# Two heads in one kernel: a weight load split in two, a bank held in the scan's later groups, and a new written-out order

## The chip, the core and the metric

The kernel runs on one core of a Trainium2 chip. The metric is the device time of one execution in microseconds (us). Three runs of the kernel before took 134.9, 135.98 and 136.2 us; their median is 135.98 us.

The core's engines each work through a list of their own, in order: TensorE (PE, with the weight loads as PEld), VectorE (DVE), ScalarE (ACT), GpSimd (POOL) and SyncE (SP). SP issues most DMA transfers, ACT and POOL some.

## What is computed

Two independent heads over sequences of 2048 rows of 448 columns, bfloat16 in and out, side by side in the output:

```
A: dt = exp(log_dt);  Lam_bar = exp(dt * Lam)                    # complex, 448 states
   Bu = x @ (((Lam_bar - 1) / Lam) * B).T
   h[t] = Lam_bar * h[t-1] + Bu[t]                               # scan over 2048 steps
   y = 2 * real(h @ C.T) + x * Dskip

B: q, k, v = split(x @ wqkv), 16 heads of 28
   logits[s, w] = q[s] . k[s - 2w] / sqrt(28),  w = 0..7         # 8 positions back, 2 apart
   o = softmax(logits) @ v,   out = o @ wo
```

## The kernel before

**How the work is cut.** Head B is cut into two halves of 1024 rows, b = 0 and 1. Its q and k are projected in blocks of 128 columns (`prep`: `first` for the two leading blocks of b = 0, in quarters; `proj` for the rest; matmuls at L494 and L453), evicted by ACT into `qk` (by the helper `copy`, L202 without and L204 with a scale), multiplied on DVE for all eight distances (`qk`, L560, tile `prods`), summed over the head's columns by PE with a selection matrix (L573), and put through a softmax (L588 on). v is projected at L673 into `ra` and later `qk`, gets its halo rows by DMA (L699, L701), and DVE forms the weighted sum (`pv`: L727 multiply, L733 add, L736 to L744 fold) in four groups. SP transposes each group (L771), PE applies `wo` (L790, L797), and the result is evicted into `ra` (L804) and stored (L807).

Head A is a chunked scan (`scan`) in seven groups m of 64 complex states, each 128 partitions high. In each group PE forms four inputs from x (L1135), two of them in a bank pair P, the odd ones in a bank each. Then a chain of small steps goes to and fro between PE and ACT: `s1` (L1152), eviction `e1` (L1156), `s2` (L1159), eviction (L1163), `s3` (L1167 to L1169), a second-level scan of five steps (L1179) with evictions `pbuf` (L1174), `s4` (L1185), and the evictions into h (L1188, L1212, L1240). DVE or ACT builds the powers `pw` that serve as weights (L1084, L1082). The outputs of A come from L1319 (seven matmuls per half tile), after a skip term that PE (L1338) or ACT (L1331, from DVE's product L1305) puts into the bank; they are stored at L1342.

**The bank of the odd term.** After `e1` has left bank 1 of a group, the carry must be added to what was in it (`s5`). The table `FIN` says how, per group, for the pair P and for this bank. "seed" means that the bank is given back after `e1`, and that ACT later copies `e1` into a bank (`back1`, L1199) on which `s5` then accumulates. "hold" means that the bank is kept from `s1` to the end of `s5` and its eviction, and no copy back is made. Before, all entries are "seed".

**What sets the order.** A planner has a list of some 610 units, each with its engine, its predecessors and the PSUM banks that it takes and gives back. The order in which the units are issued is written out as numbers in `ORDER` (a number over 1000 takes the unit's second engine), and the bank of each claim in `BANKS`. So an engine's list follows `ORDER`; an engine waits only for what its next instruction needs.

**The weights of q and k.** `loads` fetches `wqkv` in column groups a (0 to 127), b (128 to 255) and c (256 to 447), for rows 0 to 383: a on ACT's queue, b and c on SP's. The last 64 rows come in one transfer on ACT's queue (L362). `shift` then makes a copy of the weights moved by 64 partitions (`copy`: L202 on ACT, L206 on DVE), and `wm` gathers the last 64 columns of q and k (L434, DVE). For the last block the rows of k3 and q3 are copied to the other half of the partitions by DMA (`dup`, L535 and L536), on SP's queue. Eleven warm-up matmuls (L287) open PE's list.

**The tail.** The last output tile of each head is evicted in halves. The second half is shared by ACT (256 columns) and DVE (192 columns); all stores are issued by SP.

Of the kernel before, what the change touches and what calls it, by code (L numbers as in the profile page):

```python
# [16 lines left out]
D = 448  # L17
# [25 lines left out]
FIN = (("seed", "seed"),) * 7  # L43
# [32 lines left out]
]  # L76
BANKS = [
# [235 lines left out]
class PartB:  # L313
# [9 lines left out]
    def loads(self):  # L323
# [38 lines left out]
        nc.scalar.dma_start(self.wqk[0:DT, 3], self.B_wqkv[DF:D, 0:2 * D])  # L362
        nc.scalar.preload_act_table_set("natural_log_exp_and_others")
        self.u_w["a", 0] = P.add("ACTQ", 0.0, lambda: None, lat=4.8)
        self.u_wr = P.add("ACTQ", 0.0, lambda: None, lat=5.7)
        self.u_xh = {}
        for h in range(2):
            for m in range(2):
                self.u_xh[h, m] = P.add("SP", 1.33, lambda h=h, m=m: half(h, m), [self.u0], -9, lat=(3.3, 3.0, 3.2, 2.9)[2 * h + m], dma=1.0)
            c0, c1 = ((NCH, 2 * NCH), (2 * NCH, D))[h]  # L370
            self.u_w["bc"[h], 0] = P.add("SP", 0.95, lambda c0=c0, c1=c1: cols(nc.sync, c0, c1), [self.u0], -9, lat=(3.4, 3.0)[h], dma=(0.9, 1.2)[h])
# [1110 lines left out]
```

## Time and profile before

| | us |
|---|---|
| median of three runs (lowest, highest) | 135.98 (134.9, 136.2) |
| profiled execution, its own time | 135.03 |
| its span, first to last instruction | 133.3 |
| PE, DVE, ACT busy | 126.8, 113.4, 105.4 |
| POOL busy | 12.1 |
| last matmul group starts, last store is issued | 129.00, 130.56 |

The span is what the engines' records cover; 1.7 us of the execution's own time lie around it. An engine's busy time counts its instructions, not DMA issues; a matmul that is in flight counts as busy, so PE's share is no measure of its rate. In a timeline row the first number is the start, the second the length, then engine, line, operation, what it writes and reads, and in brackets how long the engine stood idle before and what released it. In the chain of waits a row names the engine that led at that time.

### The profile page before, as it was taken

The page shows a single profiled execution, that of the slowest core. Times are in us where ns is not written, and L with a number is a line of the kernel's source. Part 1 is how long each engine was busy: PE and PEld are TensorE (multiplying, and loading weights), DVE is VectorE, ACT ScalarE, POOL GpSimd, SP SyncE. Part 2 cuts the span into 40 slices and gives each one's busy share as a digit, 9 for nine tenths or more (in the row PEclk, how much of TensorE's full clock was granted, in tenths as well). Part 3 has the DMA queues.
Part 4 walks back from the last instruction along what each step waited for, and adds up shares of the span by engine and source line. Part 5 has one row for each costly group of instructions (what it writes and reads, how often), then busy time and mean ns, then how long its engine had stood idle before and what let it go on. Part 6 is the DMA issues. An engine that isn't in the chain of part 4 may idle for free.

```text
span 133.3 us, 2479 instructions
## 1 busy us (share of the span) xinstructions
PE 126.8 (95%) x921; PEld 63.4 (48%) x921; DVE 113.4 (85%) x130; ACT 105.4 (79%) x189; POOL 12.1 (9%) x28
## 2 busy tenths in 40 slices
PE   6999989999999999999999899999999999999990
PEld 2477333434546434464454255444566555545430
DVE  5256998999999999999999999999999999992011
ACT  2067968987999957879999999989999649569270
POOL 6940491000000000000000000000000000000000
PEclk9999999999999999999999999999999999999998
DMA  4999949989346758827869988006620685318642
GB/s 91 207 199 186 146 100 232 178 193 201 73 91 104 170 147 290 222 51 152 266 97 143 260 210 244 19 0 138 147 67 0 165 227 199 102 63 219 234 148 93
DMA packets 47759, 20.25 MB, mean 152 GB/s; under 512 B 38774, under 2 KB 46346, under 8 KB 47748
## 3 DMA queue, kind: packets, MB, share of 16 engines
q1 hardware_dynamic: 46676, 19.77, 64.7%
q10 hardware_dynamic: 880, 0.31, 1.2%
q8 instruction: 7, 0.11, 0.4%
q0 software_dynamic: 192, 0.03, 0.1%
q14 instruction: 4, 0.03, 0.1%
HBM read 5.18 MB, written 4.19 MB: 70 GB/s over the span
## 4 chain that ended last, share of the span: by engine, by line
PE 73%; ACT 15%; SPq 5%; DMA 3%; issue 1%; DVE 0%; ACTq 0%
PE banks L1319 16%; PE banks L1135 12%; PE banks L453 10%; PE banks L790 7%; PE banks L673 7%; PE banks L573 6%; SPq L349 4%; PE banks L1179 3%; DMA rb<-in_B_wqkv_dram 3%; ACT qk L202 2%; ACT pbuf L1174 2%; PE banks L1152 2%; ACT h L202 2%; PE banks L797 2%; ACT banks L1217 1%; SPq L360 1%
## 5 line engine op out<-in xcount | busy, mean ns | idle before, releaser
L560 DVE TENSOR_TENSOR prods<-qk 128x4096 bf16<-128x4096 bf16 (+1 forms) x18 | 31.7, 1809 | 0.3 <-ACT qk L202 0.2
L1135 PE MATMUL banks<-xaT_sb,Bcat 128*128 128x512 bf16 (+1 forms) x112 | 26.9, 381 | 0.6 <-ACT h L202 0.6
L202 ACT CAST ra<-banks 128x896 bf16<-128x896 f32 (+2 forms) x24 | 17.9, 773 | 7.8 <-PE banks L797 4.2
L202 ACT CAST qk<-banks 128x512 bf16<-128x512 f32 (+3 forms) x20 | 16.9, 843 | 3.9 <-PE banks L453 1.4
L733 DVE TENSOR_TENSOR prods<-prods 128x7168 bf16<-128x7168 bf16 x4 | 15.6, 3892 | 0.1
L727 DVE TENSOR_TENSOR prods<-ra 128x7168 bf16<-128x7168 bf16 x4 | 15.5, 3886 | 0.0
L727 DVE TENSOR_TENSOR prods<-ra,qk 128x7168 bf16<-128x7168 bf16 x4 | 15.5, 3886 | 0.1
L1319 PE MATMUL banks<-Ccat,h 128*128 128x448 bf16 x64 | 14.7, 353 | 0.0
L453 PE MATMUL banks<-rb 128*128 128x512 bf16 (+1 forms) x64 | 13.3, 379 | 0.6 <-ACT sh L960 0.6
L1135 PEld LDWEIGHTS <-Bcat 128*128 128x128 bf16 (+1 forms) x112 | 9.1, 100 | 9.7 <-issue 3.7
L673 PE MATMUL banks<-wv,rb 128*128 128x448 bf16 (+1 forms) x64 | 13.7, 354 | 0.0
L1319 PE MATMUL banks<-Ccat,qk 128*128 128x448 bf16 x48 | 11.7, 352 | 0.0
L790 PE MATMUL banks<-wo_p,rb 128*128 128x448 bf16 x48 | 10.9, 354 | 0.0
L1174 ACT CAST pbuf<-banks 128x64 bf16<-128x64 f32 (+1 forms) x42 | 9.3, 229 | 0.9 <-PE banks L1179 0.6
L1179 PE MATMUL banks<-pbuf,pw 128*128 128x64 bf16 x77 | 9.7, 235 | 0.2
L204 ACT ACTIVATE qk<-banks 128x512 bf16<-128x512 f32 (+2 forms) x10 | 8.4, 849 | 1.2 <-PE banks L453 1.0
L1179 PEld LDWEIGHTS <-pw 128*128 128x128 bf16 x77 | 6.5, 105 | 5.5 <-issue 1.9
L453 PEld LDWEIGHTS <-rb 128*128 128x128 bf16 (+1 forms) x64 | 5.1, 96 | 7.9 <-issue 2.8
L206 DVE CAST ra<-banks 128x192 bf16<-128x192 f32 x2 | 0.7, 358 | 9.2 <-ACT ra L202 9.2
L1319 PEld LDWEIGHTS <-h 128*128 128x128 bf16 x64 | 5.8, 98 | 5.3 <-issue 0.7
L1084 DVE TENSOR_TENSOR pw<-Dm,spair 128x1280 bf16<-128x1280 bf16 (+1 forms) x13 | 8.0, 664 | 0.0
L1148 ACT CAST eP<-banks 128x1024 bf16<-128x1024 f32 x7 | 7.1, 1014 | 0.9 <-PE banks L1135 0.9
(145 smaller groups left out, 201.8 us busy)
## 6 DMA issues: line engine op xcount, KB each, us to landing
out_dram<-ra SPq DMA_DIRECT2D x12, 224.0 KB, 2.3
xaT_sb<-in_A_x_dram SPq DMA_DIRECT2D x2, 448.0 KB, 4.8
out_dram<-ra SPq DMA_DIRECT2D x8, 112.0 KB, 1.7
ra<-ra SPq DMA_DIRECT2D x2, 392.0 KB, 4.1
qk<-qk SPq DMA_DIRECT2D x2, 392.0 KB, 4.1
wv<-in_B_wqkv_dram SPq DMA_DIRECT2D x2, 336.0 KB, 4.2
ra<-ra SPq DMA_DIRECT2D x1, 588.0 KB
qk<-qk SPq DMA_DIRECT2D x1, 588.0 KB, 5.6
```

What stands on the lines that cost most here:

```text
L202: nc.scalar.copy(out, in_)
L204: nc.scalar.mul(out, in_, scale)
L453: nc.tensor.matmul(out(e)[:, j0:j1], lhsT=w, rhs=self.xB[rows, b, j0:j1, c, :], start=e not in begun, stop=True, skip_group_check=True)
L560: V.tensor_tensor(p[:, :, a:a + n], q[:, t0 + a:t0 + a + n].unsqueeze(1).to_broadcast([NCH, 4, n]), bass.AP(k.tensor, k.offset, [k.ap[0], ...
L673: nc.tensor.matmul(box["ps"][:, e, 0:D], lhsT=self.xB[rows, b, jj, c, :], rhs=self.wv[rows, c, :], start=e not in begun, stop=True, skip_g ...
L727: V.tensor_tensor(out.rearrange("p (u i d h) -> p u i d h", u=4, i=4, d=DH), self.attn[b][:, r].rearrange("p (x u i) h -> p x u i h", x=2, ...
L733: V.tensor_tensor(T1, T1, T2, op=ALU.add)
L790: nc.tensor.matmul(ps, lhsT=o[:, kt + x, :], rhs=self.wo_p[:, (KT + 1) * x + kt, :], start=(kt == 0), stop=False, skip_group_check=True)
L1135: mt(ps(i), lhsT=lhsT, rhs=rhs, start=i not in begun, stop=True, **kw)
L1174: nc.scalar.copy(pb[:, dst, PAD:PAD + NCH // d], tot(a, d))
L1179: mt(tot(out, 2), lhsT=L(T * unit * k), rhs=pb[:, src, PAD - sh:PAD - sh + NCH // 2], start=False, stop=True, **kw)
L1319: nc.tensor.matmul(ps, lhsT=self.h[m][:, i, g * NCH:(g + 1) * NCH], rhs=self.Ccat[:, m, :], start=False, stop=(m == NM - 1), skip_group_ch ...
```

## The change

Six things change; the computation stays the same.

- The last 64 weight rows come in two transfers on ACT's queue: first the columns of group a (for q and k), then the rest. What needs only group a waits for the first alone.
- `FIN`: in scan groups 3 to 6 the odd term's bank is held, not seeded.
- `wm` may be gathered by ACT too, and the order gives it to ACT. One of four copies of the attention weights (`turn`) goes from ACT to DVE.
- Stores may be issued by ACT's queue too; the order does so for the very last one. The first `dup` also goes to ACT's queue.
- The last halves are evicted in one piece, by the engine that the order names (ACT).
- `ORDER` and `BANKS` are new throughout.

```
-FIN = (("seed", "seed"),) * 7
+FIN = (('seed', 'seed'), ('seed', 'seed'), ('seed', 'seed'), ('seed', 'hold'), ('seed', 'hold'), ('seed', 'hold'), ('seed', 'hold'))
...
 ORDER = [
-    22, 2, 5, 0, 1, 6, 23, 7, 1017, 4, 8, 3, 9, 39, 15, 41, 16, 40, 18, 44, 46, 43, 42, 45, 24, 25, 27, 28, 10,
+    2, 0, 1, 24, 4, 6, 7, 5, 3, 40, 16, 17, 47, 45, 46, 41, 42, 43, 44, 25, 8, 58, 60, 48, 1018, 19, 62, 9, 61,
...
         cols(nc.scalar, 0, NCH)
-        nc.scalar.dma_start(self.wqk[0:DT, 3], self.B_wqkv[DF:D, 0:2 * D])
+        src3 = self.B_wqkv[DF:D, 0:2 * D].rearrange("p (a n) -> p a n", a=2)
+        for c0, c1 in ((0, NCH), (NCH, D)):
+            nc.scalar.dma_start(w4[0:DT, 3, :, c0:c1], src3[:, :, c0:c1])
...
-        self.u_wr = P.add("ACTQ", 0.0, lambda: None, lat=5.7)
+        self.u_wr = [P.add("ACTQ", 0.0, lambda: None, lat=5.0), P.add("ACTQ", 0.0, self.zero_late, lat=6.5)]
...
-        self.u_wm = P.add("DVE", vec2(896), lambda: nc.vector.tensor_copy(
-            self.wm[:], self.wqk.rearrange("p k (a c) -> p k a c", a=2)[:, :, :, DF:D]),
+        self.u_wm = P.add(("DVE", "ACT"), (vec2(896), act(896) + 0.05), lambda eng: cx.copy(
+            eng, self.wm[:], self.wqk.rearrange("p k (a c) -> p k a c", a=2)[:, :, :, DF:D]),
...
-            wd = [[self.u_w["ab"[kt], 0], self.u_wr], self.u_w["ab"[kt], 1]]
+            wd = [[self.u_w["ab"[kt], 0], self.u_wr[kt]], self.u_w["ab"[kt], 1]]
...
-                w = P.add("ACT", act(D - 192), lambda f=ev2: f("ACT", e0=1, c1=D - 192), [us[2], v], pr)
-                w2 = P.add("DVE", vec(192), lambda f=ev2: f("DVE", e0=1, c0=D - 192), [us[2], v], pr)
-                P.add("SP", 0.45, lambda f=out: f(e0=1), [w, w2, o], pr, rel=(sl, "yb"), lat=1.1, dma=0.5)
+                w = P.add(en, (act(448), vec(448)), lambda eng, f=ev2: f(eng, e0=1), [us[2], v], pr, rel=sl)
+                P.add(*st, lambda eng, f=out: f(eng, e0=1), [w], pr, rel="yb", lat=1.1, dma=0.5)
...
-                if n < 7:
-                    v = [P.add(*en(448), e(ev, j0=1, j1=2), [us[1], u], pr - 2, rel=sl)]
-                else:
-                    v = [P.add("ACT", act(256), lambda f=ev: f("ACT", j0=1, j1=2, c1=256), [us[1], u], pr - 2),
-                         P.add("DVE", vec(192), lambda f=ev: f("DVE", j0=1, j1=2, c0=256), [us[1], u], pr - 2)]
-                P.add("SP", 0.45, lambda f=out: f(j0=1, j1=2), [*v, o], pr, rel=("ya", sl) if n == 7 else "ya", lat=1.1, dma=0.5)
+                v = [P.add(*en(448), e(ev, j0=1, j1=2), [us[1], u], pr - 2, rel=sl)]
+                P.add(*st, lambda eng, f=out: f(eng, j0=1, j1=2), v, pr, rel="ya", lat=1.1, dma=0.5)
```

The table's effect is seen in the engines' lists. Line numbers of the changed kernel differ by up to 4 from those of before.

ACT's list at the start, from the shift of group c on; `rb` holds the weights, L202 and L204 (L201 and L203 after) are the evictions of q and k, L957 to L960 (L960 to L963) the exponentials and sines of head A. Before:

```order
L202 COPY rb<-rb 64x6x192
L202 CAST qk<-banks 128x512
L204 ACTIVATE qk<-banks 128x512
L202 CAST qk<-banks 128x512
L204 ACTIVATE qk<-banks 128x512
L957 ACTIVATE ex<-karg 128x105
L960 ACT_TABLE_LOAD
L960 ACTIVATE sh<-ang,turn 128x105 x2
L204 ACTIVATE qk<-banks 128x1024
```

After:

```order
L201 COPY rb<-rb 64x6x192
L201 COPY wm<-rb 128x896
L201 CAST qk<-banks 128x512
L203 ACTIVATE qk<-banks 128x512
L203 ACTIVATE qk<-banks 128x1024
L201 CAST qk<-banks 128x512
L203 ACTIVATE qk<-banks 128x512
L960 ACTIVATE ex<-karg 128x105
L963 ACT_TABLE_LOAD
L963 ACTIVATE sh<-ang,turn 128x105 x2
L201 CAST qk<-banks 128x1024
```

The copy to `wm` has come in, and one eviction of 1024 columns has moved ahead of the table load and the sines.

ACT's list in the scan, where the fourth of the seven copies L1199 stood; L1174 (L1177) are the evictions of the second-level scan, L1163 (L1166) and L1148 (L1151) those of groups further on. Before:

```order
L202 COPY ra<-ra 128x512
L1174 CAST pbuf_118<-banks 128x64 [waits PE_49,Activation_49]
L1199 CAST banks<-e_1021 128x512 [waits Activation_49]
L1174 CAST pbuf_118<-banks 128x128 [waits PE_49]
L1163 CAST eG<-banks 128x384
```

After:

```order
L1159 CAST e_1087<-banks 128x512 [waits PE_49]
L1177 CAST pbuf_119<-banks 128x64 [waits PE_49,Activation_49] x2
L1166 CAST eG<-banks 128x384
L1177 CAST pbuf_119<-banks 128x128 [waits PE_49]
L1151 CAST eP<-banks 128x1024
```

The copy back is gone, and the other evictions follow one another in a slightly other order.

ACT's list at the very end; all rows are evictions of outputs, L1345 is a store. Before:

```order
L202 CAST ra<-banks 128x448 [waits DMAHW2_49,PE_49]
L202 CAST ra<-banks 128x896 [waits DMAHW6_49,PE_49]
L202 CAST ra<-banks 128x256
L202 CAST ra<-banks 128x448 [waits PE_49]
L202 CAST ra<-banks 128x256 [waits PE_49]
```

After:

```order
L201 CAST ra<-banks 128x448 [waits DMAHW7_49,PE_49,Activation_49]
L201 CAST ra<-banks 128x896 [waits DMAHW3_49,PE_49]
L201 CAST ra<-banks 128x448 [waits DMAHW0_49,PE_49]
L201 CAST ra<-banks 128x448 [waits PE_49] x2
L1345 DMA out_dram<-ra 128x448 [waits DMAHW5_49,Activation_49]
```

The pieces of 256 columns have become pieces of 448 (DVE's two pieces of 192 are gone), and ACT issues the last store. On PE the two matmul groups L790 and L797 of the last pair of projections stand ahead of seven L1319 matmuls, not ahead of fourteen. DVE's list has three multiplications L1305 (not two) ahead of its first L744, and one between the two L744, as before.

More of the change, by code (lines that the diff above doesn't have):

```diff
@@ L368, in loads @@
             for m in range(2):
-                self.u_xh[h, m] = P.add("SP", 1.33, lambda h=h, m=m: half(h, m), [self.u0], -9, lat=(3.3, 3.0, 3.2, 2.9)[2 * h + m], dma=1.0)
+                self.u_xh[h, m] = P.add("SP", 1.33, lambda h=h, m=m: half(h, m), [self.u0], -9, lat=(2.9, 2.7, 3.2, 2.9)[2 * h + m], dma=1.0)
             c0, c1 = ((NCH, 2 * NCH), (2 * NCH, D))[h]
@@ L388, in shift @@
             self.u_w[g, 1] = [
-                P.add(("DVE", "ACT"), (k * n / 3840.0 + 0.16, act(k * n) + 0.04), lambda eng, o=o, i=i: cx.copy(eng, o, i), [self.u_w[g, 0], self.u_wr if k == 4 else None], -8)
+                P.add(("DVE", "ACT"), (k * n / 3840.0 + 0.16, act(k * n) + 0.04), lambda eng, o=o, i=i: cx.copy(eng, o, i), [self.u_w[g, 0], self.u_wr[g != "a"] if k == 4 else None], -8)
                 for k, o, i in ((3, w[lo, 4:7, :, c0:c1], w[hi, 0:3, :, c0:c1]), (4, w[hi, 3:7, :, c0:c1], w[lo, 0:4, :, c0:c1]))]
@@ L804, in ev2, with out @@
                 cx.copy(eng, cx.yb_v[:, jb["y"], e0:e1, c0:c1], jb["ps"][:, e0:e1, c0:c1])
-            def out(j0=j0, jb=jb, e0=0, e1=2):
-                nc.sync.dma_start(self.out_b[b][:, j0 + e0:j0 + e1, :], cx.yb_v[:, jb["y"], e0:e1])
+            def out(eng, j0=j0, jb=jb, e0=0, e1=2):
+                (nc.sync if eng == "SP" else nc.scalar).dma_start(self.out_b[b][:, j0 + e0:j0 + e1, :], cx.yb_v[:, jb["y"], e0:e1])
                 if e1 == 2:
@@ L812, in pv @@
             us += [P.add("PE", pe(1, 448), rr, us[:], pr, mode="r")]
-            en = ("ACT", "DVE")
+            en, st = ("ACT", "DVE"), (("SP", "ACT"), (0.45, 0.45))
             if tail:
                 v = P.add(en, (act(448), vec(448)), lambda eng, f=ev2: f(eng, e1=1), [us[2], *cx.u_free], pr, acq="yb")
-                o = P.add("SP", 0.45, lambda f=out: f(e1=1), [v], pr, lat=1.1, dma=0.5)
-                w = P.add("ACT", act(D - 192), lambda f=ev2: f("ACT", e0=1, c1=D - 192), [us[2], v], pr)
-                w2 = P.add("DVE", vec(192), lambda f=ev2: f("DVE", e0=1, c0=D - 192), [us[2], v], pr)
-                P.add("SP", 0.45, lambda f=out: f(e0=1), [w, w2, o], pr, rel=(sl, "yb"), lat=1.1, dma=0.5)
+                P.add(*st, lambda eng, f=out: f(eng, e1=1), [v], pr, lat=1.1, dma=0.5)
+                w = P.add(en, (act(448), vec(448)), lambda eng, f=ev2: f(eng, e0=1), [us[2], v], pr, rel=sl)
+                P.add(*st, lambda eng, f=out: f(eng, e0=1), [w], pr, rel="yb", lat=1.1, dma=0.5)
             else:
                 v = P.add(en, (act(896), vec(896)), ev2, us + cx.u_free, pr, rel=sl, acq="yb")
-                P.add("SP", 0.45, out, [v], pr, rel="yb", lat=1.1, dma=1.0)
+                P.add(*st, out, [v], pr, rel="yb", lat=1.1, dma=1.0)
 class PartA:
@@ L1339, in skip, with out @@
                                      rhs=self.dg[:].rearrange("p a b -> p (a b)")[:, NCH * k:c1], skip_group_check=True)
-            def out(j=j, jb=jb, j0=0, j1=2):
-                nc.sync.dma_start(self.out_a[:, j + j0:j + j1, :], cx.ya_v[:, jb["r"], j0:j1])
+            def out(eng, j=j, jb=jb, j0=0, j1=2):
+                (nc.sync if eng == "SP" else nc.scalar).dma_start(self.out_a[:, j + j0:j + j1, :], cx.ya_v[:, jb["r"], j0:j1])
                 if j1 == 2:
@@ L1363, in outputs @@
             e = lambda f, **k: (lambda eng: f(eng, **k))
+            st = ("SP", "ACT"), (0.45, 0.45)
             if n < 5:
                 v = P.add(*en(896), e(ev), us + x + cx.u_free, pr - 2, rel=sl, acq="ya")
[L1366 removed]
+                P.add(*st, out, [v], pr, rel="ya", lat=1.1, dma=1.0)
             else:
                 u = P.add(*en(448), e(ev, j0=0, j1=1), us[:1] + x + cx.u_free, pr - 2, acq="ya")
[L1369 to L1375 removed]
+                P.add(*st, lambda eng, f=out: f(eng, j0=0, j1=1), [u], pr, lat=1.1, dma=0.5)
+                v = [P.add(*en(448), e(ev, j0=1, j1=2), [us[1], u], pr - 2, rel=sl)]
+                P.add(*st, lambda eng, f=out: f(eng, j0=1, j1=2), v, pr, rel="ya", lat=1.1, dma=0.5)
 @with_exitstack
```

10 lines of the change are left out of this document (5 added, 5 removed), and 61 rows, old and new, of tables (BANKS, ORDER).

## Prediction

> **What bounds the kernel now.** I read the engine shares first, then the busy time by stretch, the chain that ended last, and the timeline where the chain changes engine.
>
> ```profile
> PE 126.8 (95%) x921; PEld 63.4 (48%) x921; DVE 113.4 (85%) x130; ACT 105.4 (79%) x189; POOL 12.1 (9%) x28
> ```
>
> ```profile
> 60.00:70.00 10.00, 10.00 (x69) 4.89 (x68) 9.90 (x4) 9.81 (x21) 0.00 (x0) 1.00 0.72 172
> 70.00:80.00 10.00, 9.30 (x60) 4.24 (x58) 9.97 (x7) 9.86 (x21) 0.00 (x0) 1.00 0.98 204
> 80.00:90.00 10.00, 9.98 (x71) 4.91 (x70) 9.97 (x7) 9.32 (x21) 0.00 (x0) 1.00 0.32 88
> 90.00:100.00 10.00, 9.87 (x78) 5.51 (x77) 9.96 (x3) 9.80 (x24) 0.00 (x0) 1.00 0.48 117
> 100.00:110.00 10.00, 10.00 (x78) 5.91 (x76) 9.83 (x7) 6.92 (x12) 0.00 (x0) 1.00 0.51 131
> ```
>
> The columns are stretch, length, then PE, PEld, DVE, ACT and POOL, each with its instructions, then clock and DMA. The clock is full in all of them, so nothing hangs on it. From 60 to 100 us three engines are full at once: PE with 39.15 of 40, DVE with 39.80, ACT with 38.79. After 100 us ACT drops to 6.92 of 10, and PE stays full. The shares cannot say who leads between 60 and 100; the chain can.
>
> ```profile
> 64.86 1.01 ACT h L202
> ...
> 73.81 0.92 ACT h L202
> 74.77 0.81 PE banks L1135 x3
> ...
> 89.57 0.21 ACT pbuf L1174
> ...
> 94.25 0.20 ACT pbuf L1174
> 94.50 0.33 PE banks L1179 x3
> ...
> 100.13 0.20 PE banks L1338 x4
> ```
>
> ACT leads twice: from 64.86 to 74.77 (9.91 us) and from 89.57 to 94.50 (4.93 us). Of the 35.27 us from 64.86 until PE takes over for good at 100.13, that is 14.84 us, or 42%. In those stretches PE waits for scan evictions, and a microsecond off ACT is one off the end; in the others PE leads. From 100 us PE has a row of ready matmuls, and the end is PE's end plus one eviction and one store.
>
> **The change part by part.** PE's instructions are the same 921 before and after, so only PE's waits and what follows PE's end can change.
>
> *The weight rows.* One transfer of 64 rows on ACT's queue becomes two, the first with group a's columns.
>
> ```profile
> 1.82 0.53 ACTq L362 DMA_DIRECT2D rb<-in_B_wqkv_dram  x1
> 5.58 0.42 DVE L206 COPY rb<-rb 64x1024 bf16<-64x1024 bf16 x1 [0.58 <-DMA rb<-in_B_wqkv_dram]
> 5.99 1.68 PE L494 MATMUL banks<-rb 128*128 128x128 bf16 x24
> ```
>
> The only reader that waited was a DVE copy, for 0.58 us. It ended at 6.00, and the first real matmul started at 5.99, behind warm-up matmuls whose number is unchanged. Three matmuls (3/24 of 1.68, 0.21) stand ahead of the shifted rows and cover the copy. So the gain is 0, hidden by the warm-up; without that cover it would be at most 0.58. The loss is one more issue of 0.53 on ACT, which at that time waits for data: 0.
>
> *The start of the order.* On ACT one 1024-column eviction now goes ahead of the sine block, the 896-column copy to `wm` comes to ACT from DVE, and the two stores of the first `dup` move from SP's queue to ACT's.
>
> ```profile
> 15.07 1.28 ACT L960 ACT_TABLE_LOAD   x1
> 16.37 0.66 ACT L960 ACTIVATE sh<-ang,turn 128x105 f32<-128x105 f32 x2
> 16.93 1.00 ACT L204 ACTIVATE qk<-banks 128x1024 bf16<-128x1024 f32 x1
> 17.17 3.30 PE L453 MATMUL banks<-rb 64*128 64x512 bf16 x16 [0.65 <-ACT sh L960]
> 19.86 1.94 ACT L204 ACTIVATE qk<-banks 128x1024 bf16<-128x1024 f32 x2 [1.03 <-PE banks L453]
> ```
>
> ```profile
> L1331 ACT CAST banks<-xaT_sb 128x896 f32<-128x896 bf16 x4 | 3.7, 915 | 0.4 <-ACT ra L202 0.4
> L434 DVE COPY wm<-rb 128x896 bf16<-128x896 bf16 x1 | 0.4, 384 | 0.0
> ```
>
> PE waited 0.65 us there, because the eviction that frees a bank pair stood behind the table load and the sines. Now PE gets one pair earlier and meets the block one tile later. Best case: all 0.65 is saved. Worst case: ACT's additions, 0.92 for `wm` (by the 896-column copy) and two issues at 0.53 as for the weight rows, 1.98 together, less the 1.03 that ACT idled for PE just behind, cost 0.95. The two issues wait for ACT's own evictions just ahead of them; behind them queue ACT's copy of the B rows and later evictions, for which PE and DVE wait. SP's x loads come forward by two issues, 1.06. I take -0.3: the wait is pushed on rather than removed, so half of 0.65.
>
> *The held bank.* In scan groups 3 to 6 the accumulator of the odd term stays in its bank until its carry is added; before, ACT copied it back.
>
> ```profile
> L1199 ACT CAST banks<-e 128x512 f32<-128x512 bf16 x7 | 4.2, 601 | 0.0
> L202 ACT COPY ra<-ra 128x512 bf16<-128x512 bf16 x4 | 2.4, 621 | 0.0
> ```
>
> Four of seven copies go, 4 x 0.601 = 2.40 us. One of the four attention copies goes from ACT to DVE, 0.62. Together 3.02 off ACT, all in the scan. If every microsecond lay on the path the end would come 3.02 earlier; if all of it fell where PE leads, 0. ACT leads 42% of that stage, and the new order spreads the evictions anew, so I take 42%: 3.02 x 0.42 = 1.27, as -1.3. What is late next is PE itself.
>
> *The tail.* The last pair of output projections moves behind all but seven of the final matmuls, and each final half is evicted by one instruction of 448 columns, not by ACT and then DVE; the last store goes out on ACT's queue.
>
> ```profile
> 119.51 0.62 DVE L744 TENSOR_TENSOR rb<-prods 128x896 bf16<-128x896 bf16 x1
> 119.45 2.61 SPq L771 DMA_TRANSPOSE rb<-rb  x2
> 124.06 2.43 PE L790 MATMUL banks<-wo_p,rb 128*128 128x448 bf16 x12
> 129.77 0.37 ACT L202 CAST ra<-banks 128x256 bf16<-128x256 f32 x1 [0.79 <-PE banks L1319]
> 130.18 0.36 DVE L206 CAST ra<-banks 128x192 bf16<-128x192 f32 x1 [1.34 <-ACT ra L202]
> ```
>
> ```profile
> L202 ACT CAST ra<-banks 128x448 bf16<-128x448 f32 x6 | 3.2, 535 | 2.7 <-PE banks L797 2.0 <-PE banks L1319 0.8
> rb<-rb SPq DMA_TRANSPOSE x5, 3.1
> ```
>
> The two pieces ran one after the other, 129.77 to 130.54, 0.77 us; one of 448 takes 0.535: -0.2. Nothing is queued behind the store on ACT; I count its move as 0.
>
> DVE's path limits the gain. Its last L744 ended at 120.13; the second transpose, issued halfway through the 2.61, about 120.75, landed some 3.1 later, at 123.85. PE needs it behind six of the twelve matmuls, at 124.06 + 6 x 0.19 = 125.2: 1.35 to spare. Seven output matmuls fewer behind it add 7 x 0.19 = 1.3. DVE's own list before that point changes by -0.38 (`wm`), at most +0.42 (the attention copy, bounded by the 1024-column copy above) and +0.6 (one more multiplication L1305, as long as the L744 beside it): +0.6. So PE can come forward by 1.35 + 1.3 - 0.6 = 2.05 us before DVE decides.
>
> Sum: 0 - 0.3 - 1.3 - 0.2 = -1.8 us. The profiled execution took 135.03 us, of which the span is 133.3, so by it 133.2. The median of the runs, 135.98, is 0.95 above that execution; from the median the forecast is **134.2 us**.
>
> **The rivals.** *Hidden relief.* The removed copies lie outside the stretches that ACT leads:
>
> ```profile
> 81.39 0.60 ACT L1199 CAST banks<-e 128x512 f32<-128x512 bf16 x1
> 96.57 0.63 ACT L1199 CAST banks<-e 128x512 f32<-128x512 bf16 x1
> ```
>
> For it: the fourth and sixth copies start at 81.39 and 96.57, where PE leads, and DVE is as full as PE. Then only the tail is gained: 135.98 - 0.2 = 135.8. Against it: ACT is busy for 9.32 of the 10 us that lead to the second stretch, so most of what is taken out at 81.39 reaches it. A variant is that DVE, with 99.5% of 60 to 100, sets the end; then its +0.6 counts against the tail's -0.2, and the time is 136.4. The 2.05 us to spare speak against it.
>
> The Trainium skill, page Perfetto Trace Analysis, section Identifying the Most-Contended Engine, says that time is generally won on the engine with the highest occupancy, and that matmul busy time is no good measure for TensorE. By that rule DVE is the engine to look at here and nothing taken off ACT counts, so the variant's time holds; the trace agrees on DVE's occupancy, but its chain of waits passes through PE and ACT.
>
> *Held banks starve PE.* PE takes its list in order, and the tiles of the next group, of the projection and of the outputs need two neighbouring banks. A bank held through the whole second-level scan keeps a pair from being whole.
>
> ```profile
> 74.77 0.81 PE L1135 MATMUL banks<-xaT_sb,Bcat 128*128 128x512 bf16 x3 [0.58 <-ACT h L202]
> ```
>
> This row is such a wait already: the next group's matmuls stand for 0.58 us until ACT has evicted a pair. One per held group costs 4 x 0.58 = 2.3, 136.5 in all, still no difference. It decides from six: 6 x 0.58 - 1.8 = +1.7, 137.7. For it: scan, projection and outputs share eight banks, and PE is in order. Against it: the held bank needs no second claim on a bank, which the copy back did.
>
> *More than forecast.* If ACT leads the whole stage, PE gains up to the limit: 135.98 - 2.05 - 0.2 = 133.7.
>
> **How the numbers follow.** About 1% (1.36 us) is what a measurement of this kernel can tell from no change. The forecast has 0.50, and its own range is 133.7 to 135.3 (its terms between their bounds, capped by DVE); 0.36 of that lies below 134.6. More than forecast has 0.10, hidden relief with its DVE variant 0.22, held banks 0.18. So faster is 0.36 + 0.10 = 0.46, same 0.14 + 0.22 = 0.36, slower 0.18. The range goes from 132.8 (the limit, counted from the profiled execution: 135.03 - 2.25) to 137.2 (just short of six waits).
>
> **What would show it.**
>
> ```profile
> 107.63 1.01 ACT L202 CAST qk<-banks 128x1024 bf16<-128x1024 f32 x1 [1.27 <-PE banks L1231]
> ```
>
> Right: three L1199 copies; this last 1024-column scan eviction about 1.5 us earlier; ACT leading the chain for less than 14.84 us; one 448-column eviction at the end. Wrong: PE rows of L1135, L790 or L1338 that wait for ACT at new places; a DVE gap ahead of a prods multiplication; PE waiting for rb's last transpose.

## The result and the profile after

The changed kernel took 147.2 us (median of four runs, 146.3 to 148.0) where the kernel before took 135.72 in the same session: a ratio of 1.085, 95% interval 1.075 to 1.095. It is slower by 11.5 us, far outside the range forecast. Some executions of every version fell into a slower state; the medians below are of all runs, and the ratios and intervals leave the slow ones out, so a ratio can differ from the quotient of two medians.

The page of the changed kernel, engine shares and the chain by engine:

```profile
PE 128.3 (88%) x914; PEld 64.7 (45%) x921; DVE 112.8 (78%) x128; ACT 104.7 (72%) x185; POOL 10.6 (7%) x28
...
PE 67%; SPq 17%; DMA 6%; ACT 6%; issue 1%; ACTq 0%
```

The engines do the same work as before (DVE and ACT 0.6 and 0.7 us less), in a span of 144.9 instead of 133.3. Queues and transfers, SPq and DMA, now have 23% of the chain. The busy time by stretch says where:

```profile
20.00:30.00 10.00, 9.27 (x70) 3.38 (x69) 9.60 (x13) 5.28 (x7) 2.87 (x4) 1.00 0.81 136
30.00:40.00 10.00, 2.05 (x5) 0.71 (x5) 0.81 (x1) 3.98 (x6) 0.00 (x0) 0.58 0.72 154
40.00:50.00 10.00, 10.00 (x80) 4.36 (x80) 8.63 (x9) 8.59 (x9) 0.00 (x0) 0.91 0.29 56
```

From 30 to 40 us PE and DVE stand still, PE for 8 of 10 us and DVE for 9. The granted clock falls to 0.58 in that stretch and is 0.91 in the next. The waits between 20 and 50 us name three engines that stop, each waiting for the one before:

```profile
ACT ra L201 <- DMA xaT_sb<-in_A_x_dram: 10.6, 1, 10.6
DVE prods L564 <- DMA qk<-qk: 9.4, 1, 9.4
PE banks L457 <- ACT qk L203: 8.7, 1, 8.7
```

And the timeline shows how one leads to the next:

```profile
24.33 1.02 ACT L203 ACTIVATE qk<-banks 64x1024 bf16<-64x1024 f32 x1
...
31.05 9.15 SPq L871 DMA_TRANSPOSE xaT_sb<-in_A_x_dram  x7
34.02 0.58 ACTq L539 DMA_DIRECT2D qk<-qk  x1
35.39 0.54 ACTq L540 DMA_DIRECT2D qk<-qk  x1
35.97 0.56 ACT L201 COPY ra<-ra 128x448 bf16<-128x448 bf16 x1 [10.63 <-DMA xaT_sb<-in_A_x_dram]
36.44 0.54 ACT L201 CAST spair<-sfac 128x420 bf16<-128x420 f32 x1
36.88 1.02 ACT L203 ACTIVATE qk<-banks 128x1024 bf16<-128x1024 f32 x1
...
37.95 2.29 PE L457 MATMUL banks<-rb 128*128 128x512 bf16 x5 [8.68 <-ACT qk L203]
...
39.20 2.29 DVE L564 TENSOR_TENSOR prods<-qk 128x4096 bf16<-128x4096 bf16 x1 [9.36 <-DMA qk<-qk]
```

The same place in the kernel before, where SP issues the store:

```profile
23.17 1.02 ACT L204 ACTIVATE qk<-banks 64x1024 bf16<-64x1024 f32 x1
...
25.17 0.53 SPq L535 DMA_DIRECT2D qk<-qk  x1
```

In the changed kernel ACT's last eviction of the rows that `dup` copies ended at 25.35. `dup`'s two stores, now on ACT's queue, went out only at 34.02 and 35.39, and behind them ACT's next eviction began at 36.88. PE waited for the bank pair that it freed, DVE for the rows that the stores brought.

Why ACT stood for 8.7 us before an issue of 0.58 is told by the waits that the program gives to its instructions. From ACT's and from SP's list:

```
ACT  L203 ACTIVATE qk<-banks 64x1024
ACT  L539 DMA qk<-qk 64x1024 [waits DMAHW0_49,Activation_49]
ACT  L540 DMA qk<-qk 64x1024 [waits DMAHW1_49,Activation_49]
ACT  L201 COPY ra<-ra 128x7x64 [waits DMAHW2_49]

SP   L875 DMA xaT_sb<-xa_rest 64x128 [waits DMAHW7_49,DMAHW1_49]
SP   L871 DMA_TRANSPOSE xaT_sb<-in_A_x_dram 128x4x128 [waits DMAHW0_49]
SP   L871 DMA_TRANSPOSE xaT_sb<-in_A_x_dram 128x4x128
SP   L871 DMA_TRANSPOSE xaT_sb<-in_A_x_dram 128x4x128 [waits DMAHW2_49]
```

A semaphore is a counter on which an engine waits. In this program the transfers from SP's and ACT's queues use eight of them in turn (DMAHW0 to 7), and a transfer that takes one over waits until the transfer that had it last has landed. In the program's list the eight x transposes that SP issues from 31.05 on stand ahead of `dup`: they need nothing, and `dup` needs ACT's evictions. So L539 waits for the first of them and L540 for the second: issued at 31.05 and 32.37, landed just before 34.02 and at 35.32. Before, the stores stood in SP's own list, the later transposes stood behind them, and each store took over from a transfer landed long before (at 19.20 and 20.02, the first store being issued at 25.17).

The rest of the profile after, against the lines that the prediction named. The start:

```profile
6.20 0.33 PE L498 MATMUL banks<-rb 128*128 128x128 bf16 x3 [0.87 <-DMA rb<-in_B_x_dram]
```

Of the matmuls that ran as one row of 24 from 5.99 only three begin at 6.20, after a wait for x rows; the other 21 begin at 8.27 after another of 1.74, and DVE's first multiplication at 14.21 instead of 12.25. The 21 also run slower, 2.40 us for a row that takes 1.33 with one transfer (p_one_w, below). The stretch from 8 to 12 us, in the changed kernel and then in p_one_w, has the granted clock in the last column but two:

```profile
8.00:12.00 4.00, 3.73 (x34) 3.12 (x35) 1.23 (x6) 1.04 (x2) 0.71 (x4) 0.61 1.04 230
```

```profile
8.00:12.00 4.00, 4.00 (x41) 3.17 (x39) 2.87 (x12) 3.59 (x7) 0.87 (x4) 1.00 1.01 195
```

All six profiles with the new order and two transfers have 0.50 to 0.69 there, all others (the new order with one transfer, and every one with the order of before) 1.00. The scan and the end:

```profile
L1202 ACT CAST banks<-e 128x512 f32<-128x512 bf16 x3 | 1.7, 590 | 0.0
```

```profile
119.64 1.01 ACT L201 CAST qk<-banks 128x1024 bf16<-128x1024 f32 x1 [0.95 <-PE banks L1195]
...
141.62 0.53 ACT L201 CAST ra<-banks 128x448 bf16<-128x448 f32 x1 [0.47 <-PE banks L1322]
142.18 0.37 ACTq L1345 DMA_DIRECT2D out_dram<-ra  x1
```

Three copies back (L1199, now L1202) and one eviction of 448 columns at the end are there as forecast. The last 1024-column scan eviction is 12.0 us later instead of 1.5 earlier. ACT leads the chain from 55 us to the end for 6.3 us instead of 14.7.

### The profile page after: what moved, and what is told of

It reads as the page before. It is cut to its first block, busy times and chain, and to the rows that moved or that the text cites. A ratio compares the mean times of both kernels' runs of the same rounds, so it can differ in the third digit from the quotient of the medians.

```text
span 144.9 us, 2463 instructions
## 1 busy us (share of the span) xinstructions
PE 128.3 (88%) x914; PEld 64.7 (45%) x921; DVE 112.8 (78%) x128; ACT 104.7 (72%) x185; POOL 10.6 (7%) x28
## 4 chain that ended last, share of the span: by engine, by line
PE 67%; SPq 17%; DMA 6%; ACT 6%; issue 1%; ACTq 0%
PE banks L1322 15%; PE banks L1138 13%; PE banks L677 8%; SPq L871 8%; PE banks L794 7%; PE banks L457 5%; DMA rb<-in_B_x_dram 4%; PE banks L577 4%; SPq L352 4%; PE banks L1182 3%; DMA xaT_sb<-in_A_x_dram 2%; PE banks L801 2%; PE banks L1155 2%; PE banks L1195 1%; PE banks L1062 1%
## 5 line engine op out<-in xcount | busy, mean ns | idle before, releaser
L564 DVE TENSOR_TENSOR prods<-qk 128x4096 bf16<-128x4096 bf16 (+1 forms) x18 | 32.0, 1812 | 11.5 <-DMA qk<-qk 9.4
L201 ACT CAST ra<-banks 128x896 bf16<-128x896 f32 (+1 forms) x24 | 18.2, 785 | 7.4 <-PE banks L1322 2.8
L457 PE MATMUL banks<-rb 128*128 128x512 bf16 (+1 forms) x64 | 15.7, 416 | 8.7 <-ACT qk L203 8.7
L201 ACT CAST qk<-banks 128x512 bf16<-128x512 f32 (+3 forms) x20 | 16.8, 845 | 3.3 <-PE banks L1195 1.5
L457 PEld LDWEIGHTS <-rb 128*128 128x128 bf16 (+1 forms) x64 | 5.7, 104 | 16.9 <-issue 13.0
L677 PE MATMUL banks<-wv,rb 128*128 128x448 bf16 (+1 forms) x64 | 13.0, 354 | 0.0
L1177 ACT CAST pbuf<-banks 128x64 bf16<-128x64 f32 (+1 forms) x42 | 9.6, 229 | 3.9 <-PE banks L1182 2.9
L498 PE MATMUL banks<-rb 128*128 128x256 bf16 (+2 forms) x76 | 8.4, 284 | 2.6 <-DMA rb<-in_B_x_dram 2.6
L1182 PE MATMUL banks<-pbuf,pw 128*128 128x64 bf16 x77 | 10.1, 235 | 0.3
L201 ACT COPY ra<-ra 128x512 bf16<-128x512 bf16 (+1 forms) x4 | 2.4, 620 | 10.6 <-DMA xaT_sb<-in_A_x_dram 10.6
L1182 PEld LDWEIGHTS <-pw 128*128 128x128 bf16 x77 | 6.2, 105 | 6.0 <-issue 1.9
L498 PEld LDWEIGHTS <-rb 128*128 128x128 bf16 (+1 forms) x76 | 6.5, 112 | 4.7 <-issue 2.8
L203 ACT ACTIVATE qk<-banks 128x512 bf16<-128x512 f32 (+2 forms) x10 | 8.5, 858 | 0.0
```

What stands on the lines that cost most here:

```text
L201: nc.scalar.copy(out, in_)
L457: nc.tensor.matmul(out(e)[:, j0:j1], lhsT=w, rhs=self.xB[rows, b, j0:j1, c, :], start=e not in begun, stop=True, skip_group_check=True)
L498: nc.tensor.matmul(box["ps"][:, e, k, 64 * j0:64 * j1], lhsT=self.wqk[rows, c, D * k + NCH * kt:D * k + NCH * kt + NCH], rhs=self.xB[rows, ...
L564: V.tensor_tensor(p[:, :, a:a + n], q[:, t0 + a:t0 + a + n].unsqueeze(1).to_broadcast([NCH, 4, n]), bass.AP(k.tensor, k.offset, [k.ap[0], ...
L677: nc.tensor.matmul(box["ps"][:, e, 0:D], lhsT=self.xB[rows, b, jj, c, :], rhs=self.wv[rows, c, :], start=e not in begun, stop=True, skip_g ...
L1182: mt(tot(out, 2), lhsT=L(T * unit * k), rhs=pb[:, src, PAD - sh:PAD - sh + NCH // 2], start=False, stop=True, **kw)
```

## The experiments

**The theory** (A): ACT, which works in order, stands before `dup`'s stores until late x transposes of SP have landed; that would be nearly all of the loss. **Rivals:** the stores are slow because the transposes fill the DMA engines (B), or the new order of SP's loads makes the hole (C). All ratios are to the kernel before on the same chip, with 95% intervals.

**Dup on SP's queue again** (a_dup_sp).

```
 ORDER: ... 84,
-    1085, 88, 123,
+    85, 88, 123,
```

> The changed kernel with the first dup's two stores back on SP's queue, at the same place of the order. Theory A (ACT stands in order): on ACT's queue each of the two stores waits until the DMA that last used its semaphore, an x transpose that SP issues at 31 to 34 us, has landed, and ACT's evictions stand behind. It expects ACT's wait of 10.6 us and PE's of 8.7 us to be gone, DVE's wait of 9.4 us for the copied rows to fall under 1 us, and 147.2 - 8.7 = 138.5 us (137 to 139.5). Rival B (contention): the stores are slow because the x transposes fill the DMA engines, whichever queue issues them; then DVE still waits 5 us or more for the copied rows and the time stays above 143 us. Rival C (the order): the hole comes from the new order of SP's loads and ACT's copy of the B rows; then ACT's wait stays and the time is about 147 us.

139.29 us, ratio 1.014 (1.002 to 1.027), which makes it about 138. The hole is gone, as A expects and B and C do not.

**One store on each queue** (a_dup_half).

```
                 q = nc.sync if eng == "SP" else nc.scalar
-                q.dma_start(self.k3[hi, ...
+                nc.sync.dma_start(self.k3[hi, ...
                 q.dma_start(self.q3[hi, ...
```

> The changed kernel with dup's first store (the keys) on SP's queue and the second (the queries) still on ACT's. The store on SP keeps the later x transposes behind it, so the store on ACT follows a transpose that landed long before. Theory A expects no wait of ACT at the store, no hole, 138.5 us (137 to 139.5), although a store is still issued on ACT's queue among the same x loads. Rival B and rival C expect the hole to stay: 143 to 147 us.

137.85 us, 1.014 (1.009 to 1.018). Timeline of this run:

```profile
25.57 1.02 ACT L203 ACTIVATE qk<-banks 64x1024 bf16<-64x1024 f32 x1
25.58 0.53 SPq L539 DMA_DIRECT2D qk<-qk  x1
26.15 3.95 SPq L871 DMA_TRANSPOSE xaT_sb<-in_A_x_dram  x3
26.62 0.54 ACTq L540 DMA_DIRECT2D qk<-qk  x1
27.26 0.57 ACT L201 COPY ra<-ra 128x448 bf16<-128x448 bf16 x1 [0.66 <-ACT qk L203]
```

A store is issued on ACT's queue 0.03 us after the eviction that it needs, and ACT goes on 0.66 later. It is not ACT's queue as such that is dear, but what the store waits for there. The store on SP's queue keeps the transposes behind it.

**Dup on POOL's queue** (a_dup_pool).

```
-                q = nc.sync if eng == "SP" else nc.scalar
+                q = nc.sync if eng == "SP" else nc.gpsimd
```

> The changed kernel with both of dup's stores on POOL's queue, whose semaphores SP's and ACT's DMAs do not share; SP's x transposes run as far ahead as in the changed kernel. Theory A expects no wait of ACT and no hole, the copied rows there by about 31 us (issue at 25.4 and 4 to 5 us to landing, as POOL's other DMAs), DVE waiting under 2 us, and 138.5 us (136.5 to 140). Rival B expects the copied rows late (after 34 us) and over 142 us, since the transposes fill the DMA engines as before. Rival C expects about 147 us.

136.36 us, 1.0027 (0.9992 to 1.0062), just below what A expected: about 11 us of the 11.5 are gone by this edit alone (10.8 by the medians, 11.2 by the ratios). POOL's stores in this run:

```profile
25.02 0.62 POOL L539 DMA_DIRECT2D qk<-qk  x1 [2.89 <-ACT qk L201]
...
25.67 0.55 ACT L201 COPY ra<-ra 128x448 bf16<-128x448 bf16 x1
```

```profile
qk<-qk POOLq DMA_DIRECT2D x2, 128.0 KB, 3.8
```

The second row of the first fence is ACT going on at once. The second fence is from the list of DMA issues (their number, size, and median us from issue to landing): the stores land 3.8 us after their issue, while SP's transposes run as far ahead as in the changed kernel. So transposes in flight do not make the stores late by the 9 us that DVE waited (B), and their new order alone does not stop ACT (C). The Trainium skill, page DMA: Bandwidth & Descriptors, section Anatomy of one DMA — SWDGE (gpsimd) path, says that DMA engines do not wait on semaphores and that the issuing sequencer does so before it sends the transfer off; the section is on GpSimd's transfers, and the trace agrees for ACT's, with ACT's 8.7 us ahead of L539.

**That edit alone, in the kernel before** (b_dup_act): unit 84 becomes 1084 in its `ORDER`.

> The kernel before with nothing changed but the queue of the first dup's two stores: ACT's in place of SP's. Theory A expects the same hole without any other part of the change: ACT stands from about 27.7 us until a transpose that SP issues at about 33 us has landed (36 us), PE stops once its bank pairs are full, and the time is 141 to 145 us. Rival B expects a smaller loss, 136 to 139, since DMA traffic is that of before. Rival C expects no change, 135 to 136.5 us.

144.86 us, 1.059 (1.048 to 1.071). Its waits up to 50 us:

```profile
DVE prods L560 <- DMA qk<-qk: 9.9, 1, 9.9
ACT qk L202 <- DMA xaT_sb<-in_A_x_dram: 8.2, 1, 8.2
PE banks L453 <- ACT qk L202: 7.4, 1, 7.4
```

The same three rows as after the change, without any other part of it: A is shown. C fails, and B's 136 to 139 is far off.

**The split alone, in the kernel before** (b_split): its one transfer becomes the two of the change; both are waited for.

> The kernel before with nothing changed but the last 64 weight rows in two transfers instead of one (both are waited for as before, no other order). Theory S: the split makes more and smaller packets among the first loads, so weights and x rows land later; it expects the first real matmuls to stop again behind late rows, the first DVE multiplication about 1 us later than 12.25 us, and a time 0.7 to 2 us over the kernel before. Rival R: the late start of the changed kernel comes from its new order of PE's first tiles; it expects no difference over 0.5 us here.

136.38 us, 1.0075 (1.0042 to 1.0109): 1.0 us, as theory S expects, and the first matmuls do stop again. But DVE's first multiplication is only 0.26 us later (12.51), not about 1, so where the microsecond arises is not shown.

**One transfer again, with dup on POOL's queue** (p_one_w): the split undone in a_dup_pool.

> The changed kernel with dup on POOL's queue (136.36 us) and the last 64 weight rows in one transfer again. Theory S expects the first real matmuls near 6.0 us with less waiting behind them and 134.4 to 135.6 us, below the kernel before by what the scan gains. Rival R expects the start as late as with the split and 136 to 136.8 us.

135.26 us, 0.9975 (0.9943 to 1.0008): 0.5% or 0.7 us below a_dup_pool (the intervals overlap a little), against the kernel before no difference that can be told. From the list of DMA issues in the first 8 us, the four x transposes with their median us from issue to landing, in the kernel before, in b_split and in p_one_w:

```profile
rb<-in_B_x_dram SPq DMA_TRANSPOSE x4, 4.1
```

```profile
rb<-in_B_x_dram SPq DMA_TRANSPOSE x4, 5.3
```

```profile
rb<-in_B_x_dram SPq DMA_TRANSPOSE x4, 4.2
```

The median goes from 4.1 to 5.3 with the split alone and back to 4.2 without it (5.3 in the changed kernel). SP issues them at the same times within 0.2 us (0.8 to 6.1 before, 0.8 to 6.3 in b_split).

**ACT's work put back** (p_again).

```
+                    if m > 1 and n == 3:
+                        nc.scalar.copy(box["eG"][:], box["e1"][:, 0:384])
```

> The changed kernel with dup on POOL's queue (136.36 us) and, in scan groups 2 to 6, one more ACT copy of 384 columns each (about 0.49 us by L1166, 2.4 us in all, as much as the held banks took off ACT), whose result nobody reads. If 42% of ACT's time in the scan lies on the path, as the prediction took it, it costs 1.0 us: 137.4. If ACT has been taken off the path by the change, it costs under 0.4 us: 136.2 to 136.8. If ACT sets the whole stage it costs 2.4 us: 138.8.

137.29 us, 1.012 (1.008 to 1.017): 0.9 us over a_dup_pool by the medians, 1.0% or 1.3 us by the ratios. The five copies took 0.52 each, 2.6 us in all. This is the first case or a little more: a third to a half of the 2.6 us comes through.

**Dup on POOL's queue in the kernel before** (b_dup_pool): unit 84 becomes 1084, and the second queue is POOL's.

> The kernel before with nothing changed but the queue of the first dup's two stores: POOL's in place of SP's. If SP's place in the queue matters (the x loads behind dup come some us earlier and something on the path waits for them), it is 0.5 us or more faster. If nothing waits for them, the time stays within 0.5 us of the kernel before; the copied rows may land up to 1 us later, and DVE's 8.97 us of multiplications from 23.19 us cover it. ACT must show no wait at the stores, unlike with ACT's queue (144.86 us).

136.05 us, 1.0045 (1.0018 to 1.0073): 0.6 us slower, just outside what was expected. The loads that come forward bring nothing, and POOL's queue is no free place either. ACT has no wait at the stores, but one at its next copy, which began at 27.07 without a wait in the kernel before:

```profile
29.35 0.62 ACT L202 COPY xaT_sb<-xaT_sb 64x512 bf16<-64x512 bf16 x1 [1.80 <-DMA xaT_sb<-in_A_x_dram]
```

Why that load of x is there later stays open.

**Dup on SP's queue, three transposes later** (a_sp_late).

```
-    1085, 88, 123, ... 119, ... 126,
+    88, 123, 119, 126, 85, ...
```

> The changed kernel with dup on SP's queue, behind all of the first x transposes of A instead of ahead of the last three of them (SP issues the last at 25.4 us, when ACT's evictions of the rows have just ended). No other part is undone. If the place in line is all that the first dup cost, SP no longer stands still for the evictions: 135.8 to 137 us, against 139.29 with dup on SP's queue at its old place and 136.36 on POOL's. If SP's queue costs time wherever dup stands (as 1.06 us more in front of SP's later loads), it stays at 138 to 139.5.

136.68 us, 1.0090 (1.0054 to 1.0127), in the first range. SP stands in order too: in a_dup_sp it issues nothing from 22.21 to 25.72 us, with three x transposes behind, and here it issues without a gap up to the stores at 25.73. That this place is worth time is not shown, since the interval lies within that of a_dup_sp (1.002 to 1.027).

**The same with one transfer** (q_best).

> The same place of dup on SP's queue, and the last 64 weight rows in one transfer again: what is left of the change is the held banks, the order, the eviction and store at the end, the copy to wm on ACT and the attention copy on DVE. The split cost 0.7 to 1.0 us in the two kernels where it was done or undone alone; POOL's queue cost 0.6 us in the kernel before. If these add, it is 0.8 to 1.4 us below the kernel before (ratio 0.990 to 0.994). If POOL's price does not hold here, the ratio is that with POOL's queue, 0.9975.

136.17 us, 1.0018 (0.9979 to 1.0057). The split is worth 0.7% or 1.0 us a third time. Neither case comes out: the sum (0.990 to 0.994) fails, and 0.9975 lies just below the interval.

**And wm on DVE** (q_best_wm): 1039 becomes 39.

> As the run before, with the 896-column copy to wm on DVE again (0.38 us there, 0.94 us on ACT). If ACT leads at the start, it is 0.3 to 0.9 us faster than that run; if DVE, full from 22 us on, sets the pace, 0.3 us slower; if neither, no difference that can be measured.

136.41 us, 1.0045 (1.0004 to 1.0086): the interval overlaps that of q_best; no difference that can be told.

**ACT's copies cut, in the kernel before** (b_cut7).

```
-                    nc.scalar.copy(box[1], box["e1"][:])
+                    nc.scalar.copy(box[1][:, 0:64], box["e1"][:, 0:64])
```

> The kernel before with ACT's seven copies of L1199 cut from 512 columns to 64, nothing else changed: the other 448 columns of the odd accumulator are left out, so its output is not the reference's. It takes about 0.4 us off each (0.60 to 0.2), 2.8 us off ACT in the scan. The prediction's 42% gives -1.2 us (ratio 0.991); relief that stays hidden gives 0; ACT setting the whole stage gives -2 to -2.8 (ratio 0.980 to 0.985).

135.66 us, 1.001 (0.997 to 1.005): nothing, though the copies are shorter as meant:

```profile
L1199 ACT CAST banks<-e 128x64 f32<-128x64 bf16 x7 | 1.6, 227 | 0.0
```

7 x (601 - 227) = 2.6 us came off ACT. From DVE's first product of the weighted sum on, its lead in the chain fell from 14.7 to 10.4 us, and PE's rose from 60.2 to 64.3.

**DVE's additions cut, in the kernel before** (b_dve_cut).

```
-                V.tensor_tensor(T1, T1, T2, op=ALU.add)
+                V.tensor_tensor(T1[:, 0:6144], T1[:, 0:6144], T2[:, 0:6144], op=ALU.add)
```

> The kernel before with DVE's four additions of L733 cut from 7168 columns to 6144, nothing else changed (those columns are left out, so its output is not the reference's): about 0.56 us off each, 2.2 us off DVE between its first multiplication L727 and its last L744. If DVE sets the pace of that stretch (in every kernel run so far it takes 65.9 to 66.1 us from the one to the other), the stretch falls to 63.8 and the time by up to 2.2 us, less what PE is then behind: 0.5 to 2 us faster. If ACT and PE set it, as the prediction read the chain, nothing changes (within 0.4 us), as with 2.6 us less on ACT (135.66 us, ratio 1.001).

136.09 us, 1.0023 (0.9990 to 1.0056): nothing either. From the timeline, DVE's first product of the weighted sum, its last fold and PE's last matmuls, in this run and then in the changed kernel:

```profile
55.72 3.89 DVE L727 TENSOR_TENSOR prods<-ra 128x7168 bf16<-128x7168 bf16 x1
...
118.94 0.62 DVE L744 TENSOR_TENSOR rb<-prods 128x896 bf16<-128x896 bf16 x1
...
130.39 0.73 PE L1319 MATMUL banks<-Ccat,qk 128*128 128x448 bf16 x3
```

```profile
67.37 3.89 DVE L731 TENSOR_TENSOR prods<-ra 128x7168 bf16<-128x7168 bf16 x1
...
132.67 0.62 DVE L748 TENSOR_TENSOR rb<-prods 128x896 bf16<-128x896 bf16 x1
...
140.85 0.73 PE L1322 MATMUL banks<-Ccat,qk 128*128 128x448 bf16 x3
```

From the first product to the end of the last fold DVE took 63.84 us instead of 65.98 in the kernel before: the 2.1 us are off. From the first product to PE's end it was 75.40 instead of 75.58. DVE was done earlier, and PE was not.

**Two transfers by rows, in the kernel before** (b_rows).

```
+        for r0, r1 in ((0, DT // 2), (DT // 2, DT)):
+            nc.scalar.dma_start(self.wqk[r0:r1, 3], self.B_wqkv[DF + r0:DF + r1, 0:2 * D])
```

> The kernel before with the last 64 weight rows in two transfers as in the change, but cut by rows (32 whole rows each) instead of by columns: one more transfer, pieces as large as before. If small pieces are what makes the split dear (0.7 to 1.0 us), this costs nothing: within 0.3 us of the kernel before, x transposes landing after a median of about 4.1 us. If one more transfer on ACT's queue is what counts (table load and all later DMAs one place later), it costs the same 0.7 to 1.0 us, x transposes landing after about 5.3 us.

136.27 us, 1.0061 (1.0032 to 1.0091), x transposes landing after

```profile
rb<-in_B_x_dram SPq DMA_TRANSPOSE x4, 5.1
```

So it is one more transfer among the first loads that costs, not the size of its pieces. By which way it delays the transposes, and by which way that reaches the end, stays open: the first matmuls wait here for DVE's copy of the weights alone (0.50 us), and DVE's first multiplication begins at 12.12, earlier than before.

**The second dup on POOL's queue, in the kernel before** (b_dup2_pool: 1114 for 114) **and in p_one_w** (p2_one_w: 1115 for 115).

> The kernel before with the second dup's two stores on POOL's queue instead of SP's, the first left on SP's. In one run of the kernel before with shorter ACT copies DVE waited 1.6 us for these rows, in another not at all. If that wait decides between its fast and slow runs, this is 0.3 to 0.8 us faster and its runs lie closer together; if POOL's queue costs what it cost with the first dup, it is 0.3 to 0.6 us slower.

> The best version so far (ratio 0.9975: the changed kernel with the first dup on POOL's queue and the weight rows in one transfer) with the second dup on POOL's queue too. If DVE's arrival at its first multiplication of the attention output is held up by these rows in some runs, it is 0.2 to 0.8 us faster (ratio 0.992 to 0.996); if they are there in time, no difference.

135.32 us, 1.0017 (0.9983 to 1.0052), and 135.65 us, 1.0006 (0.9980 to 1.0033): no difference in either. The second dup is no cause, and no version tried beats the kernel before by more than its interval.

## Why the prediction was wrong, step by step

**The start of the order: "I take -0.3", bounds -0.65 to +0.95. This step failed.** It priced the two moved issues at 0.53 each and let them "wait for ACT's own evictions just ahead of them". They also waited for two transposes of SP. It named rightly what queues behind them on ACT; what it did not ask is what an issue waits for beyond its data. In the changed kernel that wait is 8.7 us on ACT, and the move costs about 11 us (147.2 - 136.36 = 10.8; 11.2 by the ratios); alone in the kernel before it costs 8 to 9 us (144.86 - 136.18 = 8.7; 8.1 by the ratio). The "1.06" by which SP's loads would come forward was wrong as well: they came ahead of `dup` altogether, and that made it wait. What is left of the start is a loss too. With dup on POOL's queue and the split undone the time is 0.34 us below the kernel before, while the part after DVE's first product of the weighted sum is 1.4 shorter (next but one), so the part before it is still some 1.0 us longer. About 0.4 of that is work moved ahead, which leaves 0.6: a loss where a gain was taken, within the bounds. The runs do not divide it.

**The weight rows: "the gain is 0, hidden by the warm-up", "the loss ... 0". Failed by 0.7 to 1.0 us**, in three pairs of runs (b_split, p_one_w, q_best). No gain shows: the DVE copy that had waited began at 5.58 before and at 6.66 after. And what the warm-up was to cover is not only the weights: with the extra transfer the x rows land 1.2 us later in the median, past its end, and the first matmuls wait for them or for that copy (0.87 and 1.74 us for x in the changed kernel; 0.40 and 0.31 for x and 0.82 for the copy in b_split). In the new order the granted clock falls as well, to 0.61 from 8 to 12 us; in the order of before it does not (1.00), and the split costs as much. The step looked at the readers of the split rows, not at the other transfers in flight.

**The held bank and the stage after: "I take 42%", -1.3. The size comes out near, by luck; the reason fails.** From DVE's first product to PE's end it is 75.3 to 75.8 us in all eight profiles with the order of before, and 74.1 to 74.4 in all nine profiles with the new order and no work added, the changed kernel's 74.21 among them. That is 75.58 - 74.21 = 1.37 us less. Not all of it is gained: before, 76 of the 77 small matmuls L1179 stand behind DVE's first product, after (L1182) 67. Nine take about 0.4 us of PE's list, an estimate from a row of three at 54.49 whose follower starts at 54.63, and they are only done earlier.

Taking 2.6 us off ACT alone gave 0.27 in this stretch (75.31 in b_cut7), no more than these profiles differ among themselves, and no time. Adding 2.6 us in the new order cost 0.8 (74.93 against 74.12), and 0.9 to 1.3 in the whole. So ACT's time has no fixed price of 42%: off, it is worth a tenth at most; on, a third to a half. What the other 1.0 us comes from is not shown. It may be the new order, or the held bank by another way than ACT's time, since it also takes a step out of each group's chain; holding the banks alone was not tried.

What this says of the reading of before: the chain gave ACT 14.84 us, and that share was taken as a price, because "in those stretches PE waits for scan evictions". The busy time in just these two stretches (columns as in the prediction) says otherwise:

```profile
64.86:74.77 9.91, 9.21 (x64) 4.49 (x63) 9.84 (x5) 9.90 (x22) 0.00 (x0) 1.00 0.83 165
89.57:94.50 4.93, 4.79 (x33) 2.36 (x31) 4.93 (x2) 4.93 (x12) 0.00 (x0) 1.00 0.43 95
```

PE is busy for 14.0 of the 14.84 us. As far as busy time tells, a faster ACT could save PE some 0.8 us there, not 14.84; from DVE's first product to its end PE is idle 0.86 us before and 0.66 after. When ACT was relieved, PE took over the lead. When DVE was relieved, PE's end stayed. The prediction's own sentence, "what is late next is PE itself", was right, and sooner than it thought.

**The tail: -0.2.** From PE's last matmul to the end of the span it was 3.57 us before (133.3 - 129.73) and 3.32 after (144.9 - 141.58). Right within what the profiles differ: it is 3.5 to 3.7 in all with the order of before, 3.3 to 3.6 in those with the new one.

**The DVE limit of 2.05 us** was not put to the test, since the end never came forward. The forecast's own range was also too narrow for its terms: at their worst bounds they add to 0.95 - 0.2 = +0.75, 136.7 us, where it ended at 135.3.

**The rivals.** Hidden relief was right on ACT's copies (b_cut7), with all else against it. Its variant with DVE, and the rule that the prediction took from the Trainium skill, page Perfetto Trace Analysis, section Identifying the Most-Contended Engine, that time is won on the engine with the highest occupancy, do not fit: DVE was 99.5% busy from 60 to 100 us and 2.1 us less there gave nothing. Starved PE was right in the sign alone: PE's long wait is in the projections at 29 us, not in a held group. No rival, and no chance, stood for a store that waits at its issue. Of the three "wrong" signs one came, the gap ahead of a multiplication (L564, 9.36), in a place that none of the sums had looked at; PE's wait for ACT came at L457 (8.68), a line that was not among those named.

Of the 11.5 us lost, then: about 11 for dup on ACT's queue, 0.7 to 1.0 for the split, and the rest of the change together within 0.6% of nothing, with the stretch after DVE's first product 1.4 us shorter and the one before it longer by nearly as much.

## What to carry to other kernels

Moving a transfer to a compute engine's queue cost that engine whatever the transfer waited for before it was issued, and that included the semaphore that it took over: read the waits of the issue in the program's list, find when their releasers land, and count everything that is queued behind. One more transfer among the first loads was not free, although its data were not urgent: the urgent ones landed later. Where three engines are full at once, the chain's leader is not the price: look first how long the next engine in the chain is idle in those stretches, then take time off one engine without changing the order, and see whether the end moves, before counting on it.

## What the runs showed that was not expected

- Once issued, `dup`'s stores of 128 KB took a median of 2.4 us to land from SP's queue in the kernel before, 3.1 from ACT's in a_dup_half, 3.7 from ACT's in the changed kernel and 3.8 from POOL's in a_dup_pool. The queue makes a difference of 1.4 us there, not of 10.
- The first matmuls' waits of 0.87 and 1.74 us go with a granted clock of 0.61 in the four us from 8 on, and the row of 21 behind them takes 2.40 us instead of 1.33. So waits much shorter than the hole at 30 us can go with a lower clock; the 0.38 and 0.85 us of p_one_w did not.
- With PE idle for 8.7 us the granted clock is 0.58 in that stretch and 0.91 in the next (0.68 and 0.97 in b_dup_act, idle for 7.4). In the runs without the hole the stretch from 30 to 40 us has 1.00.
- Between runs of one kernel the place of DVE's first product moves by 1 us and more (54.15 in the kernel before, 55.83 in b_cut7, whose list is the same up to there; there DVE waited 1.6 us for the second dup). A single profiled execution is no base for a difference of 1 us.
